# Attention and two MLPs on one core: load places given back earlier, more places, conversions planned further behind their loads

## The chip, the cores and the metric

One core of one Trainium2 chip runs the whole program: one launch, all inputs in HBM, the result back to HBM. The metric is the device time in microseconds (us), median over runs. TensorE (PE) multiplies, VectorE (DVE) and ScalarE (ACT) do element work, SyncE (SP) issues most DMAs, ACT issues the rest, GpSimd (POOL) does one reduction in the attention stage. Each engine works through its own instructions in program order.

## The reference

```python
def phi(x):
    proj = np.einsum('bhsd,df->bhsf', x, w_phi)
    proj = proj - np.max(np.abs(proj), axis=-1, keepdims=True)
    return np.concatenate([np.exp(proj), np.exp(-proj)], axis=-1)
q_p, k_p = phi(q), phi(k)                       # q, k, v: (4, 8, 576, 64), fp32; w_phi: (64, 128)
kv  = np.einsum('bhsf,bhsd->bhfd', k_p, v)
num = np.einsum('bhsf,bhfd->bhsd', q_p, kv)
den = np.einsum('bhsf,bhf->bhs', q_p, np.sum(k_p, axis=2))[..., None] + 1e-06
x = (num / den) as (2304, 512)
h = x @ moe_w_in;   x = np.maximum(0.01 * h, h) @ moe_w_out       # first MLP, 512 -> 2048 -> 512
h = x @ moe2_w_in;  g = h * np.tanh(softplus(h)); out = g @ moe2_w_out   # second MLP
```

The four MLP weights are float64 (the others are float32); the kernel turns them into float32 on the chip, as bit patterns.

## The kernel before

**Stages.** Attention comes first. Then the first product of the first MLP, here stage A: 8 pairs of 128 hidden rows (f = 0..7) times two halves of the tokens (sb), 16 items, each made in a Strassen-like form from seven block products. A product (`prod`, L677) is six matmuls of 128x512: every fp32 operand is split into a high and a low part, and three matmuls stand for one. `cycle(n)` (L953) writes out item n: seven products with a call of `work()` behind each. Behind each f comes `c_item`, the leftover tokens, with two more calls. Then the second product of the first MLP, stage B: 72 steps (`l2_step`), each two halves of six matmuls with a `work()` behind each (the eight steps of the leftover tokens have twelve matmuls of 256 columns a half). Then the second MLP, stage C.

**Weights.** A unit is 128 x 512 float64 numbers, 512 KB. `Loads.load` (L115) issues the next unit's DMA on SP into a load place, the tile `stage`, of which there are two, whenever one is free in the planner's books. `conversion` (L130) makes float32 of it: `clamp` (two DVE steps, L137 and L139), `scale` (one ACT step, L143), `join` (two DVE steps, L148 and L150); the load place is given on at the end of `join`. The result lies in one of three word places, tile `c`. Of the 64 units 7 are converted during attention, 31 in the order of stage A (`l1_order`: six pairs of the first MLP's input weights, and 19 others that are stored as float32 in HBM, `scr`, by `to_store`), and 26 in the order of stage B (`l2_order`: 16 of the second MLP's input weights that go straight into their final place, `direct`, and 10 that are stored). `from_store` fetches stored units back and splits them into their final place (`into_home`).

**The planner.** The order of the side work is fixed while the program is built. `work()` (L646) advances a counter of products, `pos`, adds `rate` to a budget of DVE microseconds, and lets up to four active chains (`Chain`, L620) each issue one stage if the budget is positive, the stage's `gate` is open and its `ok` holds. A chain at the head of the queue starts only when it may, and those behind it wait. `landed(u)` (L841) holds a conversion back until `LAND` = 3 products after its load was issued in the books; what the load then does on the chip the planner doesn't know. `need(mark)` issues work by force until a mark is reached, without heeding budget or `LAND`; `drain()` empties the queue by force, ahead of the last products of stage A and ahead of step 55 of stage B. A matmul that needs a DVE or ACT result stands behind whatever these engines were given earlier: the sum `g` of `tail5` (L747), `join_w` (L752), the copy `seed_y` (L700), and in stage B the low part `gl` (L95).

Of the kernel before, what the change touches and what calls it, by code (L numbers as in the profile page):

```python
# [10 lines left out]
F32 = mybir.dt.float32  # L11
# [12 lines left out]
def attention_two_mlps_kernel(  # L24
# [40 lines left out]
    CS, LAND = 3, 3  # L65
# [41 lines left out]

    class Loads:


        def __init__(self, units):
            self.units, self.at, self.stage, self.when, self.pos = units, 0, {}, {}, [0]

        def load(self, ahead=1):
            while self.at < len(self.units) and len(self.stage) <= ahead:  # L115
                which, m, x = self.units[self.at]
                self.at += 1
                stg = gp.tile([P, DM, 2], I32, tag="stage", name="stage")
# [8 lines left out]
                self.when[which, m, x] = self.pos[0]  # L127

    def conversion(u, then):

        box = {}

        def clamp():
            loads.load()
            stg = box["s"] = loads.stage[u]
            c = box["c"] = gp.tile([P, DM], F32, tag="c", name="c", bufs=CS)
            nc.vector.tensor_scalar(out=c, in0=stg[:, :, 1].bitcast(F32), scalar1=F64_TOP, scalar2=-F64_TOP,  # L137
                                    op0=ALU.min, op1=ALU.max)
            nc.vector.tensor_scalar(out=stg[:, :, 0], in0=stg[:, :, 0], scalar1=29, scalar2=None,  # L139
                                    op0=ALU.logical_shift_right)  # L140

        def scale():
            nc.scalar.activation(out=box["c"], in_=box["c"], func=AF.Copy, scale=2.0 ** -112)  # L143

        def join():
            stg, c = box["s"], box["c"]
            e = stg[:, :, 0]
            nc.vector.scalar_tensor_tensor(out=e, in0=stg[:, :, 1], scalar=-(1 << 31), in1=e,  # L148
                                           op0=ALU.bitwise_and, op1=ALU.bitwise_or)
            nc.vector.scalar_tensor_tensor(out=c.bitcast(I32), in0=c.bitcast(I32), scalar=3, in1=e,  # L150
                                           op0=ALU.logical_shift_left, op1=ALU.bitwise_or)
            del loads.stage[u]
            loads.load()
            then(c)

        return clamp, scale, join
# [7 lines left out]
    def fetch(u):  # L164
        c = gp.tile([P, DM], F32, tag="c", name="f", bufs=CS)
        nc.sync.dma_start(out=c, in_=scr[u])
        return c
# [74 lines left out]
    with tc.manual_schedule():  # L242
# [253 lines left out]
        def attention(n):  # L496
# [48 lines left out]
            if n == PAIRS - 1:  # L545
# [4 lines left out]
        ATT = {1: ((0, 0, 0), keep), 2: ((0, 1, 0), keep), 5: ((0, 0, 1), store), 7: ((0, 2, 0), keep),  # L550
               8: ((0, 3, 0), keep), 15: ((0, 1, 1), store), 16: ((0, 2, 1), store)}
        HERE, EARLY, EACH = 4, 1, 3
# [3 lines left out]
        for f in range(2, NF + 1):  # L556
# [13 lines left out]
            5: lambda: low(*w_all(0, 2, 3)),  # L570
# [7 lines left out]
            15: lambda: low(*w_all(1, 2, 3)),  # L578
# [10 lines left out]
        }  # L589

# [18 lines left out]
        gd, free, undone, pos, tokens, rate = {}, set(), set(), [0], [0.0], [1.3]  # L609
        queue, active, sent = [], [], []  # L610
        loads.pos = pos
# [34 lines left out]
        def work(force=False):  # L646
            pos[0] += 1
            while sent:
                sent.pop(0)()
            tokens[0] = min(tokens[0], 0.0) + rate[0]  # L650
            for x in list(active):
                x.step(force)
            active[:] = [x for x in active if x.stages]
            while queue and len(active) < 4 and not any(x.open() for x in active) and (force or queue[0].begin <= pos[0]):
                x, n = queue[0], len(queue[0].stages)
                x.at = -9
                x.step(force)
                if len(x.stages) == n:
                    return
                queue.pop(0)  # L660
                if x.stages:
                    active.append(x)

        def need(*mark):
            while mark in undone:
                work(True)
# [70 lines left out]
        def leaky(key, h, g=None):  # L737
            g = staged() if g is None else g
# [61 lines left out]

        c_part = lambda: cw + [XC]
        x1 = lambda o: (lambda: x_part(1, o))

        def row(cost, *todo, mark=None):
            def f():
# [22 lines left out]
              row(1.22, lo_(x1(T4)), mark=("x", 1, T4)))  # L828

        held = []

        def room(force=False):
            return len(held) < CS or held[-CS][0]

        def hold():
            held.append([False])
            return held[-1]

        def landed(u):  # L841
            def ok(force):
                loads.load()
                return room() and u in loads.stage and (force or pos[0] >= loads.when[u] + LAND)
            return ok

        def conv_stages(u, last=True):

            box = {}
            c, s, j = conversion(u, lambda x: box.update(out=x))  # L850

            def c_():
                box["h"] = hold()
                c()
            return box, [Stage(0.85, c_, ok=landed(u), last=last), Stage(0.0, s), Stage(1.38, j)]

        def drop(box, f=None):
            def g():
                if f is not None:
                    f()  # L860
                box["h"][0] = True
            return g

        def w_chain(f, begin):
# [13 lines left out]
            c1.after = 1  # L878
            chain(c0, Stage(0.85, both(s0.f, c1.f), ok=c1.ok, last=False), Stage(1.38, both(j0.f, s1.f)), Stage(1.38, both(j1.f, got)),
# [7 lines left out]
        def to_store(u):  # L887
            box, st_ = conv_stages(u)
            j = st_[2]
            f = j.f  # L890
            j.f = drop(box, lambda: (f(), store(u)(box["out"])))
            chain(*st_)
# [18 lines left out]
        def into_home(u, box):  # L911
            def h():
                home[u] = home_of(u)
                high(home[u] + [box["out"]])

            return [Stage(0.0, h), Stage(0.69, drop(box, lambda: low(home[u] + [box["out"]])), ("o",) + u)]
# [5 lines left out]
        def from_store(u, begin=0):  # L922
            box = {}

            def get():
                box["h"] = hold()
                box["out"] = fetch(u)
            h, l = into_home(u, box)
            h.after = LAND
            chain(Stage(0.0, get, ok=room, last=True), h, l, begin=begin)  # L930
# [76 lines left out]
        def load_g(s):  # L1007
# [4 lines left out]
            else:  # L1012
                if (s - LAST) % 2 == 0:
                    raw2[0] = gp.tile([P, 2, MAIN], F32, tag="stage", name="raw2")
# [113 lines left out]
        def mish(g, done):  # L1128
# [19 lines left out]
            if new:  # L1148
                if g % 2 == 0 or pair[0] is None:
                    pair[0] = gp.tile([P, 2, MAIN], F32, tag="stage", name="u")  # L1150
# [20 lines left out]
            if new:  # L1171
                r0 = gp.tile([P, MAIN], F32, tag="c", name="r", bufs=CS)
# [36 lines left out]
        for x in items[2:]:  # L1209
            if x[0] == "w" or n == 1:  # L1210
                cycle(n)
                n += 1
                if n == len(it) - 1:
                    for s in range(6):
                        load_g(s)
# [15 lines left out]
        splits(-1)  # L1231
        box2 = {}

        def swap(m):
# [3 lines left out]
            if m + CS < M:  # L1238
                box2[m + CS] = fetch(out2[m + CS])

        def l2_step(s):
            emit_y(s, 0, 1)
            work()
            emit_y(s, 2, 3)
            splits(s)
            if s < LAST + 4:
                load_g(s + 6)
            elif (s - LAST) % 2 == 0:
                load_g(s + 6)
                load_g(s + 7)  # L1250
# [4 lines left out]
        for s in range(NS):  # L1255
            if s == LAST - 1:
                drain()
            if s == LAST:
                for m in range(CS):
                    box2[m] = fetch(out2[m])  # L1260
# [45 lines left out]
```

## Time and profile before

| | |
|---|---|
| median of 3 runs | 1025.89 us (1025.8 to 1028.55) |
| the profiled execution | 1024.99 us, of which the trace's span is 1022.9 us |
| PE busy | 962.8 us, 94% |
| DVE busy | 722.6 us, 71% |
| ACT busy | 529.8 us, 52% |
| POOL busy | 68.7 us, 7% |
| DMA | 108.11 MB, 106 GB/s over the span |
| chain that ended last, by engine | PE 55%, DMA 16%, DVE 12%, issue 2%, ACT 1% |
| stage A, first to last matmul | 182.5 to 394.0 us |
| stage B up to its last conversions | 394.0 to about 550 us |

The busy shares are means over stages with different limits, so the stages are to be read one by one. A busy PE is one with a matmul in flight; it can run at the full or at half of its clock, which the row PEclk tells.

### The profile page before, as it was taken

What the parts mean: (1) busy time and instruction counts of PE and PEld (TensorE: products, weight loads), DVE (VectorE), ACT (ScalarE), POOL (GpSimd) and SP (SyncE); (2) the same over time, 40 slices, a digit from 0 to 9 for tenths busy, and PEclk for the clock granted to TensorE, in tenths of its full rate; (3) what the DMA queues carried; (4) which work ended last, traced back from release to release, by engine and by line L of the source; (5) the groups of instructions that cost most, each with busy time, mean ns of one, the idle gap of its engine ahead of it and who ended that gap; (6) DMA issues with size and microseconds to landing.
All of it is one profiled execution on the core that took longest, in us unless ns stands there. A gap on an engine that the chain in (4) does not pass through costs nothing.

```text
span 1022.9 us, 16911 instructions
## 1 busy us (share of the span) xinstructions
PE 962.8 (94%) x6645; PEld 810.4 (79%) x6645; DVE 722.6 (71%) x1282; ACT 529.8 (52%) x898; POOL 68.7 (7%) x36
## 2 busy tenths in 40 slices
PE   8999999997888879888799999999999999999998
PEld 7889998775776768766687887888888988888886
DVE  7888996765666624675665355978876888868976
ACT  6888886653544434443423344545544555545543
POOL 4434341000000000000000000000000000000000
PEclk9999999998998989999998999999999999999999
DMA  7524411265666775555576361000100100001001
GB/s 197 141 74 136 130 46 48 100 221 190 202 215 214 236 252 187 165 170 177 153 242 215 106 184 31 1 1 1 42 1 1 42 1 21 1 1 42 1 0 42
DMA packets 87246, 108.11 MB, mean 106 GB/s; under 512 B 29312, under 2 KB 54272, under 8 KB 87168
## 3 DMA queue, kind: packets, MB, share of 16 engines
q1 hardware_dynamic: 65696, 68.90, 22.6%
q10 hardware_dynamic: 21472, 38.15, 11.2%
q8 instruction: 52, 0.85, 0.3%
q14 instruction: 26, 0.21, 0.1%
HBM read 75.04 MB, written 31.98 MB: 105 GB/s over the span
## 4 chain that ended last, share of the span: by engine, by line
PE 55%; DMA 16%; DVE 12%; issue 2%; ACT 1%; ACTq 0%; DVEq 0%; SPq 0%
PE a L98 9%; PE a L100 9%; PE b L98 9%; PE a L99 9%; PE b L100 9%; PE b L99 9%; DMA stage<-in_moe_w_in_dram 8%; DMA stage<-in_moe_w_out_dram 7%; DVE stage L148 3%; DVE c L150 2%; DMA f<-scr 2%; DVE gl L95 1%; PE outs L434 1%; DVE stage L139 1%; DVE c L199 1%
## 5 line engine op out<-in xcount | busy, mean ns | idle before, releaser
L100 PE MATMUL a<-win,wi 128*128 128x512 f32 (+1 forms) x320 | 117.7, 368 | 0.0
L99 PE MATMUL a<-win,wi 128*128 128x512 f32 (+1 forms) x320 | 117.7, 368 | 0.0
L98 PE MATMUL a<-win,wi 128*128 128x512 f32 (+1 forms) x320 | 117.7, 368 | 0.0
L100 PE MATMUL b<-wo,gl 128*128 128x512 f32 x288 | 112.3, 390 | 1.0 <-DVE gl L1164 1.0
L98 PE MATMUL b<-wo,gh 128*128 128x512 f32 x288 | 112.2, 389 | 0.0
L99 PE MATMUL b<-wo,gh 128*128 128x512 f32 x288 | 112.1, 389 | 0.0
L143 ACT ACTIVATE c<-c 128x512 f32<-128x512 f32 x64 | 40.4, 632 | 101.9 <-DVE c L137 99.8
L95 DVE TENSOR_TENSOR gl<-raw,gh 128x512 fp32r<-128x512 f32 x72 | 49.5, 689 | 58.6 <-ACT gh L94 51.2
L137 DVE TENSOR_SCALAR c<-stage 128x512 f32<-128x512 f32 x64 | 27.2, 424 | 85.7 <-DMA stage<-in_moe_w_in_dram 48.9
L1146 ACT ACTIVATE gh<-u 128x512 fp32r<-128x512 f32 x72 | 45.5, 633 | 70.7 <-PE b L99 63.9
L99 PE MATMUL b<-gl,wo 128*128 128x512 f32 (+1 forms) x192 | 69.7, 363 | 7.0 <-DVE gl L95 7.0
L394 POOL PARTITION_ALL_REDUCE qm<-qd x32 | 68.5, 2189 | 90.8 <-ACT qd L389 77.2
L1173 ACT ACTIVATE r<-e,two 128x512 f32<-128x512 f32 x72 | 51.7, 718 | 36.2 <-DVE e L1158 36.2
L100 PE MATMUL b<-gh,wo 128*128 128x512 f32 (+1 forms) x192 | 69.3, 361 | 0.0
L98 PE MATMUL b<-gh,wo 128*128 128x512 f32 (+1 forms) x192 | 69.2, 360 | 0.0
L94 ACT ACTIVATE gh<-raw 128x512 fp32r<-128x512 f32 x72 | 43.5, 623 | 49.3 <-PE b L100 21.8
L98 PEld LDWEIGHTS a<-win,wi 128*128 128x128 f32 x320 | 60.3, 188 | 10.3
L99 PEld LDWEIGHTS a<-win,wi 128*128 128x128 f32 x320 | 60.3, 188 | 10.3
L100 PEld LDWEIGHTS a<-win,wi 128*128 128x128 f32 x320 | 60.3, 188 | 10.0
L1142 ACT ACTIVATE e<-a 128x512 f32<-128x512 f32 x72 | 43.0, 597 | 47.8 <-PE a L100 26.6
L99 PE MATMUL a<-gl,wo 128*128 128x512 f32 x128 | 53.5, 418 | 11.9 <-DVE gl L95 11.8
L100 PEld LDWEIGHTS b<-wo,gl 128*128 128x128 f32 x288 | 54.1, 188 | 13.0 <-DVE gl L1164 1.8
(219 smaller groups left out, 2391.7 us busy)
## 6 DMA issues: line engine op xcount, KB each, us to landing
gd<-g ACTq DMA_DIRECT2D x72, 256.0 KB, 2.8
raw<-gd ACTq DMA_DIRECT2D x72, 256.0 KB, 3.0
stage<-in_moe_w_in_dram SPq DMA_DIRECT2D x32, 512.0 KB, 4.5
stage<-in_moe_w_out_dram SPq DMA_DIRECT2D x32, 512.0 KB, 4.4
scr<-c SPq DMA_DIRECT2D x32, 256.0 KB, 4.8
f<-scr SPq DMA_DIRECT2D x32, 256.0 KB, 2.9
qn<-in_q_dram SPq DMA_DIRECT2D x16, 256.0 KB, 4.5
vmain<-in_v_dram SPq DMA_DIRECT2D x32, 128.0 KB, 3.0
```

The lines of the kernel that those rows point to most:

```text
L94: nc.scalar.activation(out=hi, in_=src, func=AF.Copy)
L95: nc.vector.tensor_tensor(out=lo, in0=src, in1=hi.bitcast(F32), op=ALU.subtract)
L98: nc.tensor.matmul(out=o, lhsT=wh_, rhs=xh, start=start, stop=False, **kw)
L99: nc.tensor.matmul(out=o, lhsT=wh_, rhs=xl, start=False, stop=False, **kw)
L100: nc.tensor.matmul(out=o, lhsT=wl_, rhs=xh, start=False, stop=stop, **kw)
L137: nc.vector.tensor_scalar(out=c, in0=stg[:, :, 1].bitcast(F32), scalar1=F64_TOP, scalar2=-F64_TOP, op0=ALU.min, op1=ALU.max)
L143: nc.scalar.activation(out=box["c"], in_=box["c"], func=AF.Copy, scale=2.0 ** -112)
L148: nc.vector.scalar_tensor_tensor(out=e, in0=stg[:, :, 1], scalar=-(1 << 31), in1=e, op0=ALU.bitwise_and, op1=ALU.bitwise_or)
L394: nc.gpsimd.partition_all_reduce(qm, qd, P, bass_isa.ReduceOp.absmax)
L1142: nc.scalar.activation(out=e0, in_=h0, func=AF.Exp)
L1146: nc.scalar.activation(out=hi2, in_=u2, func=AF.Copy)
L1173: nc.scalar.activation(out=r0, in_=e0, func=AF.Ln, bias=two)
```

## The change

The load place is given on at the end of `clamp` instead of `join`: for conversions in the stages A and B the step L148 (the low bits) moves into the same stage and writes into a second word place instead of back into the load place; the next load is issued right there. Two more load places and four more word places are cut out of tiles that held the tokens of the second half (`x2`, `x3`), from the time that those are split until product 98 (the load places until 84), and single tiles are lent later (`lh`, `a7`). A conversion needs two open word places. `LAND` goes from 3 to 6. The rates go from 1.3 to 1.15 (stage A) and from 1.0 to 0.9 (stage B). The `drain()` at the end of the cycles and the later queueing of stage B's units go: all chains are queued at once, with gates on places that stage A still uses. Some ACT and DMA issues are put one or two products later, and in stage B `splits` comes between the two halves of a step.

```diff
-    CS, LAND = 3, 3
+    CS, LAND = 3, 6
+    class Places:            # keeps the books of load and word places
+        def open(self, of):
+            return [x for x in of if x.tile is None and self.pos[0] < x.until]
+        def room(self, n):
+            return len(self.open(self.words)) >= n
+        def closed(self, close):
+            return self.pos[0] >= close and not any(x.close == close and x.tile is not None for x in self.words + self.stages)
...
+        def low_bits():
+            stg = box["s"]
+            e = box["e"] = places.take(places.words) if early else stg[:, :, 0]
+            nc.vector.scalar_tensor_tensor(out=e.bitcast(I32) if early else e, in0=stg[:, :, 1], scalar=-(1 << 31),
+                                           in1=stg[:, :, 0], op0=ALU.bitwise_and, op1=ALU.bitwise_or)
+            if early:
+                loaded()
+        def loaded():
+            places.drop(loads.stage.pop(u))
+            loads.load()
...
+            if early:
+                low_bits()                     # at the end of clamp()
...
-            del loads.stage[u]                 # at the end of join()
-            loads.load()
+            if early:
+                places.drop(e)
+            else:
+                loaded()
...
-            sent.append(lambda: nc.scalar.dma_start(out=gd[key], in_=g))
+            later(1, lambda: nc.scalar.dma_start(out=gd[key], in_=g))
...
-            leaky((2 * x["f"] + 1, 2 * x["sb"] + 1), c, c)
+            later(1, lambda: leaky((2 * x["f"] + 1, 2 * x["sb"] + 1), c, c))
...
+        def more_places():
+            for x in range(2):
+                t = place("x2_%d" % x, F32, 2, DM, name="more")
+                places.words += [places.Word(lambda t=t, i=i: t[:, i], CLOSE) for i in range(2)]
+                places.stages.append(places.Word(lambda x=x: place("x3_%d" % x, I32, DM, 2, name="stage"), CLOSE, CLOSE - 14))
...
-                return room() and u in loads.stage and (force or pos[0] >= loads.when[u] + LAND)
+                return places.room(n) and u in loads.stage and (force or pos[0] >= loads.when[u] + LAND)
...
-            return box, [Stage(0.85, c_, ok=landed(u), last=last), Stage(0.0, s), Stage(1.38, j)]
+            return box, [Stage(1.53, c, ok=landed(u), last=last), Stage(0.0, s), Stage(0.69, j)]
...
-            h.after = LAND
+            h.after = LAND - 2                 # a fetched unit
...
+            chain(*st_, Stage(0.0, drop(box), after=LAND - 1))     # a stored unit keeps its word place
...
-            from_store(out1[m])
+            from_store(out1[m], CLOSE)
+        for u in out1[HERE:]:
+            from_store(u)
+        for u in l2_order:
+            (to_store if u[2] == 1 else direct)(u)
...
-                free.update((it[n]["f"], i) for i in parts)
+                later(2, lambda: free.update((it[n]["f"], i) for i in parts))
...
-        drain()
-        for u in out1[HERE:]:
-            from_store(u)
-        for u in l2_order:
-            (to_store if u[2] == 1 else direct)(u)
...
-        rate[0] = 1.0
+        rate[0] = 0.9
...
             emit_y(s, 0, 1)
+            splits(s - 1)
             work()
             emit_y(s, 2, 3)
-            splits(s)
```

## Rows read from the trace of the kernel before

**Rows 1.** The page: forty slices of the span, PE busy and granted clock, in tenths.
```profile
PE   8999999997888879888799999999999999999998
PEclk9999999998998989999998999999999999999999
```

**Rows 2.** Stretches by stage: busy us and instructions of each engine, PEclk, DMA share, GB/s.
```profile
182.50:394.00 211.50, 184.09 (x829) 148.52 (x830) 124.56 (x223) 100.07 (x171) 0.00 (x0) 0.94 0.62 204
394.00:550.00 156.00, 135.99 (x634) 111.93 (x633) 98.86 (x180) 60.26 (x106) 0.00 (x0) 0.93 0.60 185
550.00:640.00 90.00, 89.04 (x393) 73.43 (x392) 42.38 (x67) 35.00 (x59) 0.00 (x0) 1.00 0.41 121
640.00:1022.90 382.90, 379.21 (x1762) 317.04 (x1760) 306.32 (x516) 189.95 (x304) 0.00 (x0) 1.00 0.04 13
```

**Rows 3.** PE's waits in stage A: us in total, times, longest.
```profile
PE b L98 <- ACT b L700: 10.4, 4, 5.2
PE b L98 <- DVE g L747: 7.9, 4, 2.9
PE a L98 <- ACT x L203: 4.7, 2, 4.0
PE b L98 <- DVE b L752: 1.9, 4, 1.1
PE a L100 <- DVE a L207: 1.4, 1, 1.4
PE a L100 <- DVE x L207: 1.0, 2, 0.6
```

**Rows 4.** PE's waits from 394 to 550 us, stage B.
```profile
PE a L99 <- DVE gl L95: 11.8, 8, 3.2
PE b L99 <- DVE gl L95: 7.0, 3, 3.5
PE a L98 <- ACT gh L94: 1.2, 1, 1.2
```

**Rows 5.** DVE's waits from 180 to 405 us, the longest two.
```profile
DVE c L137 <- DMA stage<-in_moe_w_in_dram: 26.2, 10, 3.6
DVE c L137 <- DMA stage<-in_moe_w_out_dram: 20.3, 12, 2.6
```

**Rows 6.** DVE's waits from 405 to 550 us, the longest two.
```profile
DVE c L137 <- DMA stage<-in_moe_w_in_dram: 22.7, 7, 4.5
DVE c L137 <- DMA stage<-in_moe_w_out_dram: 16.5, 9, 3.0
```

**Rows 7.** The tile stage: conversion steps (ns, min/median/max) and its loads' landing.
```profile
L137 DVE TENSOR_SCALAR c<-stage x64: 417/426/431, 23.3 to 547.6; 128x512 f32<-128x512 f32 x64
L139 DVE TENSOR_SCALAR stage<-stage x64: 420/422/427, 23.6 to 548.0; 128x512 int32<-128x512 int32 x64
L148 DVE SCALAR_TENSOR_TENSOR stage<-stage x64: 683/686/702, 30.9 to 550.3; 128x512 int32<-128x512 int32 x64
L150 DVE SCALAR_TENSOR_TENSOR c<-c,stage x64: 691/693/698, 31.6 to 551.0; 128x512 int32<-128x512 int32 x64
...
DMA to landing us min/median/max: 3.5/4.4/7.6
```

**Rows 8.** Timeline of DVE, stage B: start, us, line, [idle before, releaser].
```profile
431.28 0.43 DVE L137 TENSOR_SCALAR c<-stage 128x512 f32<-128x512 f32 x1 [4.49 <-DMA stage<-in_moe_w_in_dram]
...
487.07 0.43 DVE L137 TENSOR_SCALAR c<-stage 128x512 f32<-128x512 f32 x1 [3.36 <-DMA stage<-in_moe_w_in_dram]
```

**Rows 9.** Timeline of PE, stage A.
```profile
198.29 0.39 PE L98 MATMUL a<-s,a 128*128 128x512 f32 x1
...
203.05 0.39 PE L98 MATMUL b<-s,a 128*128 128x512 f32 x1
...
370.11 0.80 PE L98 MATMUL b<-v,x 128*128 128x512 f32 x1 [5.19 <-ACT b L700]
```

**Rows 10.** The stretch of 25 us with most DMA.
```profile
350.00:375.00 25.00, 19.81 (x90) 16.32 (x89) 13.39 (x24) 10.00 (x19) 0.00 (x0) 0.87 0.82 265
```

More of the change, by code (lines that the diff above doesn't have):

```diff
@@ L106, in attention_two_mlps_kernel, with __init__, take, drop @@
     scr = {}
+    class Places:
+        class Word:
+            def __init__(self, make, close=1 << 20, until=None):
+                self.make, self.close, self.until, self.tile, self.since = make, close, until or close, None, 0
+        def __init__(self):
+            self.pos, self.clock = [0], 0
+            self.words = [self.Word(lambda i=i: place("c%d" % i, F32, DM, pool=gp, name="c")) for i in range(CS)]
+            self.stages = [self.Word(lambda i=i: place("st%d" % i, I32, DM, 2, pool=gp, name="stage")) for i in range(2)]
+        def open(self, of):
[4 more added lines that the diff above has]
+            return self.pos[0] >= close and not any(x.close == close and x.tile is not None for x in self.words + self.stages)
+        def take(self, of):
+            x = min(self.open(of), key=lambda x: x.since)
+            x.tile = x.make()
+            return x.tile
+        def drop(self, t):
+            x = [x for x in self.words + self.stages if x.tile is t][0]
+            self.clock += 1
+            x.tile, x.since = None, self.clock
+    places = Places()
     class Loads:
         def __init__(self, units):
-            self.units, self.at, self.stage, self.when, self.pos = units, 0, {}, {}, [0]
-        def load(self, ahead=1):
-            while self.at < len(self.units) and len(self.stage) <= ahead:
+            self.units, self.at, self.stage, self.when = units, 0, {}, {}
+        def load(self):
+            while self.at < len(self.units) and places.open(places.stages):
                 which, m, x = self.units[self.at]
                 self.at += 1
-                stg = gp.tile([P, DM, 2], I32, tag="stage", name="stage")
+                stg = places.take(places.stages)
                 if x == 0:
@@ L126, in load, with conversion @@
                 self.stage[which, m, x] = stg
-                self.when[which, m, x] = self.pos[0]
-    def conversion(u, then):
+                self.when[which, m, x] = places.pos[0]
+    def conversion(u, then, early=False):
         box = {}
+        def low_bits():
[8 more added lines that the diff above has]
+            loads.load()
         def clamp():
@@ L162, in store, with fetch @@
         return f
-    def fetch(u):
-        c = gp.tile([P, DM], F32, tag="c", name="f", bufs=CS)
+    def fetch(u, at=None):
+        c = places.take(places.words) if at is None else place("c%d" % at, F32, DM, pool=gp, name="f")
         nc.sync.dma_start(out=c, in_=scr[u])
@@ L589, in attention_two_mlps_kernel, with free_pair @@
         }
+        def free_pair(f):
+            for i in range(2):
+                places.drop(kept.pop((0, 2 * f + i, 0)))
         def extra(n, at):
@@ L797, in attention_two_mlps_kernel @@
         head2(0)
+        def more_places():
[3 more added lines that the diff above has]
+                places.stages.append(places.Word(lambda x=x: place("x3_%d" % x, I32, DM, 2, name="stage"), CLOSE, CLOSE - 14))
+        places.words.append(places.Word(lambda: place("lh", F32, DM, pool=late[0], name="more"), CLOSE2))
         c_part = lambda: cw + [XC]
@@ L860, in g @@
                     f()
-                box["h"][0] = True
+                places.drop(box["out"])
             return g
@@ L1149, in mish @@
                 if g % 2 == 0 or pair[0] is None:
-                    pair[0] = gp.tile([P, 2, MAIN], F32, tag="stage", name="u")
+                    pair[0] = place("st%d" % (g // 2 % 2), F32, 2, MAIN, pool=gp, name="u")
                 u0 = pair[0][:, g % 2]
@@ L1230, in attention_two_mlps_kernel @@
         c_item(NF - 1, lambda: (tail3(n - 1), work()), work)
-        splits(-1)
+        work()
+        free.add("l1")
+        places.words.append(places.Word(lambda: place("a7", F32, DM, name="more")))
         box2 = {}
```

88 lines of the change are left out of this document (43 added, 45 removed).

## The prediction

> **What bounds the kernel now.** I read the slices of the page first. PE is full from the 24th slice on and at full clock there; the thin place is the middle, slices 7 to 22, where its share falls to 7 or 8 tenths and the granted clock dips too [rows 1]. By stages: from 550 us on PE is busy 468.3 of 472.9 us at clock 1.00, so nothing outside PE can shorten that; stage A (211.5 us) has clock 0.94, stage B's first part (156 us) 0.93 [rows 2]. So the loss lies in these two, and I ask the waits of PE there. In A they sum to 10.4 + 7.9 + 4.7 + 1.9 + 1.4 + 1.0 = 27.3 us [rows 3], in B to 11.8 + 7.0 + 1.2 = 20.0 us [rows 4]. All name an ACT or DVE step as releaser. One step back, DVE: in the same stretches it stood 26.2 + 20.3 = 46.5 us [rows 5] and 22.7 + 16.5 = 39.2 us [rows 6] at one instruction, L137, the first step of a conversion, waiting for its load. DVE works in order, so the sum, join or low part that PE needs was queued behind a conversion written out before its load had landed. ACT's `seed_y` comes late the same way: it stands behind a `scale` that waits for that L137. DVE is not full: 124.6 of 211.5 us and 98.9 of 156 us [rows 2].
>
> A product is short beside a load. Matmuls start (203.05 - 198.29) / 21 = 0.227 us apart [rows 9], so six are 1.36 us, and `LAND` = 3 products are 4.1 us. A load lands 3.5 to 7.6 us after its issue, median 4.4 [rows 7], and its issue on the chip comes later than in the books, since it waits for the `join` before it. More than half are late by construction.
>
> There is a second bill. In the same slices the granted clock falls below 1 [rows 1], that is, PE spends part of them at the lower of its two levels (1.2 instead of 2.4 GHz). The clock of 0.94 over 211.5 us is 0.06 x 211.5 = 12.7 us lost in A, and 0.07 x 156 = 10.9 us in B [rows 2]. So what stands above an unhindered PE is 27.3 + 12.7 = 40.0 us in A and 20.0 + 10.9 = 30.9 us in B, 70.9 us in all; the span could fall to 1022.9 - 70.9 = 952 us, and no further, since the rest is PE's.
>
> **The change, part by part.**
>
> *Six products instead of three.* Six are 8.2 us, above the longest landing seen, 7.6 us [rows 7]. Since the next load's issue is now written right behind the last reader of its place, the eight microseconds count from the issue itself, not from the books two stages earlier. Where a conversion is not forced, L137 no longer waits. That removes the cause of the 85.7 us of DVE's waits [rows 5, 6]; PE's gain is only its own 70.9.
>
> *Load place back after L148.* The DVE work per unit stays the same four steps, 0.426 + 0.422 + 0.686 + 0.693 = 2.23 us [rows 7], and so does the planner's price (0.85 + 1.38 before, 1.53 + 0.69 after). L148 now writes a dense word place and L150 reads one; the trace has no such row, so bounds: between 0.42 (the single-input steps L137, L139) and 0.70, that is a gain of at most 57 x 2 x 0.27 = 31 us of DVE time, or a loss of nothing. I take no change, as these are two-input steps of the same size, and neither lies on the path once DVE has idle time. What moves is 0.69 us from one product to another: the stage becomes one run of 0.43 + 0.42 + 0.69 = 1.53 us, which can delay a waiting `g` or `gl` by up to 1.53 us. PE asks for `g` two products (2.7 us) after it could be made, so this hides. If that cover is gone (DVE already behind by over 1.2 us), it costs up to 0.7 us a conversion.
>
> *How fast units can go then.* With `LAND` = 6 a load place turns round in six products, 8.2 us. In B there are two places, so a unit each 4.1 us. Before, ten units between the two rows of stage B took 487.07 - 431.28 = 55.8 us, 5.6 us each [rows 8]. So the longer hold is still a faster loop, as the wait and the two stages of holding are gone. 26 units take 107 us. They start when the twelve fetched units ahead of them are through (four of them at a time, four to six products each, the first four fetched ahead), some 14 products or 19 us into B, and so end at 126 us; the `drain()` ahead of step 55 stands at 55 x 2 x 1.36 = 150 us. In A, 31 units in 15 x 7 + 7 x 2 + 5 = 124 products are one per four; four places allow one per 1.5, two allow one per 3. Both suffice.
>
> *Rates.* By the planner's prices A needs about 31 x 2.22 + 6 x 4.18 for the parts of six pairs + 16 for the tokens' splits + 3 for four fetched units = 113 us of DVE, and 124 products at 1.15 give 143. B needs 26 x 2.22 + 28 x 0.69 = 77 us, 86 products at 0.9, of 110 up to the drain. So the lower rates make nothing late by themselves, and DVE gets at most 1.15 + 1.3 / 7 = 1.34 us per product of 1.36, the sums of a cycle included.
>
> *The drain at the end of A goes.* It forced fetches in a row; PE's longest wait in A, 5.19 us at 370.11, lies there [rows 9] and is in the 40 us already. *ACT's issues a product later, `splits` between the halves:* same instructions, off the path; nothing, within 1 us either way per stage.
>
> *DMA.* The same bytes. A moves 204 GB/s x 211.5 us = 43 MB [rows 2]; in 180 us that is 240 GB/s at a share of about 0.73. The densest stretch did 265 GB/s at 0.82 [rows 10], so there is room. But up to four loads can be in flight. Scaling that stretch to a full share, 265 / 0.82 = 323 GB/s, four loads of 524 KB take 6.5 us; still under 8.2. Here a rule of the Trainium skill speaks against the change: "DMA: Bandwidth & Descriptors", section "Issuing engines are not separate DMA queues", says that all DMAs end on the same 16 engines and interleave, so more of them in flight bring no more bandwidth and each lands later. With that page's limit of HBM per core, 358 GB/s (its "Specifications"), four loads would be an estimated 5.9 us. No row of before shows how four loads share; by that estimate, too, the sum stays as it is, as 5.9 us is under six products.
>
> *Sum.* I do not take all 70.9. Small waits of the chain PE-ACT-DVE-PE within a cycle stay, a few loads land late beside stores, and each long remainder brings some half clock. I choose that a fifth stays: 8 of 40 in A, 6 of 31 in B. Gain 57 us: span 1022.9 - 57 = 966, with the 2.1 us around the span 968. The profiled execution lies 0.9 us under the median, so the median is 969 us.
>
> **The rivals.**
>
> 1. *Only A gains.* B keeps two load places, and its conversions, `gl` and fetches share one DVE. If units run late there, `drain()` forces the rest and PE waits as before. For it: half of B's gain hangs on 24 us of slack before the drain. Against: the turn of 4.1 us against 5.6. Time: 1025.9 - 32 = 994.
>
> 2. *Loads stretch each other in A.* Four in flight, beside stores and `gd`, land after 8 us instead of 4.4, so L137 waits on. For: the median landing of 4.4 us is for two places. Against: the bytes are the same, and the 6.5 us above. The rule of the Trainium skill cited above would have it so, if its estimate were larger. Only B gains: 1025.9 - 25 = 1001.
>
> 3. *It doesn't do what it says.* The books run ahead of the chip; word places run out (each conversion needs two, a stored one keeps its word for seven products), and `need` forces the steps of before. DVE then waits at L137 as now: 1026.
>
> 4. *Slower: the pairs of stage A come late.* A pair needs four open words at once, and it must be complete when its item's first product is written out. If stored units hold the words, `need` forces the pair with nothing beside it: a load of 4.4 us, two conversions of 2.23 and a split of about 1.2, some 10 us, plus about 2 us of half clock behind so long a wait. Six pairs make 72 us against a gain of 57: 1041. It decides from the fifth pair on. For: two of the lent places close at product 98, load places at 84, before the last pair is done. Against: a pair starts 14 to 19 products (19 to 26 us) ahead of its need, and up to seven words are open then.
>
> **How the numbers follow.** Forecast 0.64 (969, its own range 955 to 982); rival 1 0.14 (994), rival 2 0.08 (1001), rival 3 0.06 (1026), rival 4 0.08 (1041). The floor is 952 + 3 = 955. The range runs from 954 to 1004: it holds the forecast, both half gains, and leaves out rivals 3 and 4 with 0.14 and some of the forecast's tails. The DVE bounds shift nothing in it, as DVE is off the path where loads are in time, and its 0.7 us a conversion (57 x 0.7 = 40 us, if every one is exposed) stays within it. About 0.3%, 3 us, is what a measurement tells from no change: faster 0.86 (forecast, rivals 1 and 2), same 0.06, slower 0.08.
>
> **What would show it.** Right: L137's waits for the load fall from 46.5 and 39.2 us to under 10 together; PE's waits in A and B to some 15 us; the granted clock to 0.98 or more in both; A about 180 us and B's conversions with PE full; from the first product of the second MLP on, all as before. Landing times up to 8 us and no `drain` stall ahead of step 55. Wrong: L137 still waits in A (rival 2), only in B (rival 1), or PE waits at the first product of an item for a weight's low part (rival 4).

## The result, and the profile after

The changed kernel takes 953.44 us (median of 4 runs, 952.49 to 955.93) against 1025.85 us, a ratio of 0.9298 (95% interval 0.9267 to 0.9328). The forecast was 969 with a range of 954 to 1004: the direction was right, the gain larger than forecast (72.4 us against 57), and the median lies 0.6 us under the range.

The page of the kernel after: span, slices of PE and its clock, and the chain that ended last, by engine.

```profile
span 954.0 us, 16891 instructions
PE   8999999999999989999999999999999999999998
PEclk9999999999999989999999999999999999999999
PE 85%; ACT 1%; DVE 1%; DMA 0%; issue 0%; ACTq 0%; DVEq 0%
```

The thin stretch of [rows 1] is gone but for one slice, the 15th. DMA and DVE, 16% and 12% of the chain before, are at 0% and 1%. The stretches of the kernel after, with the columns of [rows 2], cut where stage A ends (357.8 us) and at the last wait of PE (570.6 us):

```profile
182.50:357.80 175.30, 171.09 (x828) 144.31 (x829) 124.39 (x223) 99.57 (x170) 0.00 (x0) 0.98 0.75 251
357.80:550.00 192.20, 192.20 (x938) 163.08 (x937) 129.72 (x226) 86.69 (x149) 0.00 (x0) 1.00 0.66 202
570.60:954.00 383.40, 379.66 (x1762) 317.57 (x1762) 306.70 (x516) 190.19 (x305) 0.00 (x0) 1.00 0.04 13
```

Stage A took 211.5 us [rows 2] and takes 175.3: 36.2 us won. Its DVE work is the same, 124.4 us. PE is busy all through stage B. Both kernels have a last wait of PE, for the second MLP's first `gl`; here it is before and after, in the timeline of PE (start, us, line, [idle before, releaser]).

```profile
639.54 0.50 PE L100 MATMUL b<-wo,gl 128*128 128x512 f32 x1 [0.96 <-DVE gl L1164]
```

```profile
570.65 0.50 PE L100 MATMUL b<-wo,gl 128*128 128x512 f32 x1 [0.95 <-DVE gl L1223]
```

From there to the end both take 383.4 us (1022.9 - 639.54, 954.0 - 570.65), so nothing was won in stage C. Stage B up to there went from 639.5 - 394.0 = 245.5 to 570.6 - 357.8 = 212.8 us: 32.7. Together 68.9 us, the difference of the two spans. (The medians differ by 72.4: the profiled execution after lies 2.5 us above its median, the one before 0.9 under.) The waits of PE in stage A that are left (in stage B there is none up to that last one), against [rows 3, 4]:

```profile
PE b L98 <- DVE g L808: 2.5, 1, 2.5
PE b L98 <- ACT b L760: 1.3, 1, 1.3
PE a L98 <- ACT x L253: 0.4, 1, 0.4
```

And DVE's wait for loads, which was 85.7 us [rows 5, 6], with the landing times of the loads ([rows 7] before):

```profile
DVE c L182 <- DMA stage<-in_moe_w_out_dram: 0.6, 1, 0.6
...
DMA to landing us min/median/max: 3.6/4.5/7.1
```

Over all loads the landing is no shorter than before. In stage A its median even rose, from 4.5 to 5.1 us, as more loads are in flight. What changed is when loads are issued and when they are asked for.

### The profile page after: what moved, and what is told of

Same layout as the page of the kernel before. It is cut to its first block, busy times and chain, and to the rows that moved or that the text cites. A ratio compares the mean times of both kernels' runs of the same rounds, so it can differ in the third digit from the quotient of the medians.

```text
span 954.0 us, 16891 instructions
## 1 busy us (share of the span) xinstructions
PE 937.2 (98%) x6645; PEld 800.6 (84%) x6645; DVE 722.4 (76%) x1282; ACT 530.0 (56%) x898; POOL 68.7 (7%) x36
## 3 DMA queue, kind: packets, MB, share of 16 engines
q10 hardware_dynamic: 21472, 38.15, 11.9%
## 4 chain that ended last, share of the span: by engine, by line
PE 85%; ACT 1%; DVE 1%; DMA 0%; issue 0%; ACTq 0%; DVEq 0%
PE b L98 14%; PE b L100 14%; PE b L99 14%; PE a L98 14%; PE a L100 13%; PE a L99 13%; PE outs L484 1%; PE kvp L461 1%; DMA gd<-g 0%; PE a L377 0%; PE xt L509 0%; PE kvp L464 0%; PE kvp L513 0%; ACT g L800 0%; PE outs L489 0%
## 5 line engine op out<-in xcount | busy, mean ns | idle before, releaser
L1232 ACT ACTIVATE r<-e,two 128x512 f32<-128x512 f32 x72 | 51.7, 718 | 36.1 <-DVE e L1217 36.1
L98 PE MATMUL b<-gh,wo 128*128 128x512 f32 (+1 forms) x192 | 68.2, 355 | 0.0
L100 PE MATMUL b<-gh,wo 128*128 128x512 f32 (+1 forms) x192 | 68.0, 354 | 0.0
L98 PEld LDWEIGHTS b<-wo,gh 128*128 128x128 f32 x288 | 54.1, 188 | 11.1
L99 PEld LDWEIGHTS b<-wo,gh 128*128 128x128 f32 x288 | 54.1, 188 | 10.9
L1223 DVE TENSOR_TENSOR gl<-u,gh 128x512 fp32r<-128x512 f32 x72 | 49.5, 688 | 9.2 <-ACT gh L1205 9.2
```

What stands on the lines that cost most here:

```text
L98: nc.tensor.matmul(out=o, lhsT=wh_, rhs=xh, start=start, stop=False, **kw)
L99: nc.tensor.matmul(out=o, lhsT=wh_, rhs=xl, start=False, stop=False, **kw)
L100: nc.tensor.matmul(out=o, lhsT=wl_, rhs=xh, start=False, stop=stop, **kw)
L1223: nc.vector.tensor_tensor(out=lo2, in0=u2, in1=hi2.bitcast(F32), op=ALU.subtract)
L1232: nc.scalar.activation(out=r0, in_=e0, func=AF.Ln, bias=two)
```

## Experiments

The theory behind the forecast, D: six products between load and conversion take the waits away. Its rival, R: the rate at which load places come free. The first four runs test them; after them come other theories, as each was needed. All medians are against the kernel before on the same chip (1024.4 to 1026.1 us). "DVE" is DVE's waits for loads and "PE" all waits of PE, from 182 us to the end of stage B, in one profiled run each; the kernel before has 85.7 and 48.3, the kernel after 0.6 and 5.2.

| run | what | median us | ratio (95%) | DVE | PE |
|---|---|---|---|---|---|
| e1 | before, six products | 1010.21 | 0.984 (0.982 to 0.987) | 36.1 | 42.8 |
| e2 | after, three products | 953.94 | 0.930 (0.928 to 0.932) | 3.2 | 4.9 |
| e3 | after, two load places | 966.70 | 0.942 (0.940 to 0.944) | 3.4 | 15.1 |
| e4 | after, place back at join | 961.83 | 0.937 (0.935 to 0.939) | 4.6 | 11.2 |
| e5 | e2 and e3 | 957.90 | 0.936 (0.934 to 0.939) | 21.0 | 8.6 |
| e6 | e2 and e4 | 952.08 | 0.930 (0.927 to 0.932) | 3.2 | 4.2 |
| e7 | e2, e3 and e4 | 958.43 | 0.937 (0.935 to 0.939) | 10.8 | 8.3 |
| e8 | e7, old rates | 955.77 | 0.934 (0.932 to 0.936) | 16.1 | 6.1 |
| e9 | e8, conversion's old form | 1015.63 | 0.991 (0.988 to 0.994) | 81.2 | 44.6 |
| e10 | e9, three words | 1017.93 | 0.994 (0.991 to 0.996) | 84.0 | 48.2 |
| e11 | e10, drain back | 1018.11 | 0.993 (0.991 to 0.995) | 85.2 | 46.0 |
| e12 | after, splits later | 950.07 | 0.928 (0.924 to 0.931) | 0.3 | 2.7 |
| e13 | e8, low bits in place | 977.61 | 0.953 (0.951 to 0.956) | 43.2 | 18.9 |
| e14 | e8, low bits in join | 966.21 | 0.941 (0.938 to 0.944) | 28.5 | 12.8 |
| e15 | after, conversion's old form | 954.16 | 0.930 (0.927 to 0.933) | 33.2 | 5.6 |
| e16 | e9, new prices | 978.24 | 0.954 (0.952 to 0.955) | 42.5 | 21.5 |
| e17 | e9, two words in the books | 1006.19 | 0.982 (0.979 to 0.984) | 72.0 | 40.4 |
| e18 | before, new prices | 1000.47 | 0.975 (0.974 to 0.977) | 53.8 | 34.6 |

### The distance alone, and without it (e1, e2)

```diff
-  ... (force or pos[0] >= loads.when[u] + LAND)      # e1, in the kernel before
+  ... (force or pos[0] >= loads.when[u] + 6)
-  ... (force or pos[0] >= loads.when[u] + LAND)      # e2, in the changed kernel
+  ... (force or pos[0] >= loads.when[u] + 3)
```

> The kernel before with one number changed: a conversion waits for six products behind its load's issue, not three; two load places, given back at the end of join. Theory D (the distance between load and conversion is what took DVE's waits away, places matter little): DVE's waits for loads fall from 46.5 and 39.2 us to under 15 together, time 960 to 975, what stays being the two drains. Theory R (the rate of the loads matters as much): a place now turns in six plus two products, a unit per four products or 5.4 us, which is no faster than the 5.6 us of before; units fall behind, the drains and the weights' needs force them, waits at L137 come back in lumps there; 985 to 1020.

> The changed kernel with the distance put back to three products (4.1 us), all else as changed. Theory D: a load lands 4.5 us (median) behind its issue and three products are 4.1, so most of 57 conversions wait 0.5 to 3 us; DVE's waits for loads are 40 us or more and the time 970 to 1000. Theory R: the places carry the change, the waits stay under 15 us, time under 960.

e1 gains 15.6 us of 72, e2 loses nothing. So six products are not needed in the changed kernel, and alone they are not enough for the whole gain: D is wrong as the cause. R's range for e1 (985 to 1020) holds. But the two stages of e1 differ (columns of [rows 2], cut at the end of stage A and at PE's last wait):

```profile
182.50:411.30 228.80, 187.79 (x832) 150.93 (x831) 126.07 (x224) 101.82 (x171) 0.00 (x0) 0.88 0.57 189
411.30:623.60 212.30, 211.40 (x1023) 178.51 (x1022) 140.93 (x246) 95.89 (x165) 0.00 (x0) 1.00 0.60 187
```

Stage B takes 212.3 us, as in the changed kernel (212.8): there the distance alone brings the whole gain, and PE waits nowhere between 420 and 620 us. Stage A takes 228.8 us, 17.3 more than before. Its waits of PE lie elsewhere than before (timeline of PE):

```profile
247.82 0.80 PE L98 MATMUL a<-v,x 128*128 128x512 f32 x1 [7.80 <-ACT x L203]
250.38 0.80 PE L100 MATMUL a<-v,x 128*128 128x512 f32 x1 [1.33 <-DVE x L207]
253.65 0.80 PE L98 MATMUL a<-v,x 128*128 128x512 f32 x1 [1.21 <-ACT x L203]
```

These are the first products of an item, waiting 10.3 us in all for weights that come late; three such rows come again from 308 and from 369 us on. It is the place of the forecast's rival 4 and its 10 us of waiting, in a kernel where a load place turns in eight products; the half clock with it (0.88 over the stage, 0.94 before) costs more than the 2 us a pair put there.

### Places and their return in the books (e3 to e8)

```diff
-                places.stages.append(places.Word(lambda x=x: place("x3_%d" % x, ...), CLOSE, CLOSE - 14))   # e3
-                loaded()          # e4: at the end of low_bits()
+            loaded()              # e4: at the end of join(), always
-  tokens, rate = [0.0], [1.15]    ...    rate[0] = 0.9      # e8
+  tokens, rate = [0.0], [1.3]     ...    rate[0] = 1.0
```

> The changed kernel without the two lent load places: two places throughout, given back behind L169, six products. Theory D: two places turned in six products give a unit per three products, and stage A needs one per four; time 953 to 958. Theory R: stage A loses the loads in flight; a pair and the three stored units behind it come late, need forces them, time 965 to 985.

> The changed kernel with the load place given back at the end of join (two products later) instead of behind L169; four places up to product 84, then two, six products. Theory D: 953 to 960, a unit per two products in A; in B a unit per four products, so that some two to four of 26 are left for the drain ahead of step 55, which forces them for a few us. Theory R: stage B runs at 5.4 us a unit like before and PE waits there again, 970 to 990.

e3 met R's range by its lower end: pairs come late near 245 us (6.4 us of PE's waits), and the last wait of stage A grew from 2.5 to 4.9 us. e4 fell between the two ranges: 8 us longer, of which 5.4 + 0.9 us are two waits of PE at 518 to 520 us, the forced units ahead of step 55 that D had put at "a few us".

> The changed kernel with two load places and three products; early give-back and all else as changed. After the first runs: distance did nothing while four places were there. Theory B (the books: in stage B the budget, 0.9 us a product against 2.91 us a unit, spaces the loads by itself; in stage A spare places do): stage B stays free of waits; stage A has forced pairs as with two places and six products, or fewer since a conversion may start sooner; 955 to 968. Theory D' (with two places a load is fresh when it is used, so distance binds): DVE waits 1 to 2 us at most conversions of A, over 25 us in all, time 975 or more.

> The changed kernel with three products and the load place given back at the end of join; four places. Theory B: four places still let loads run ahead in A, so A is as changed; in B a place given back two products or more later turns more slowly, some units are left for the drain ahead of step 55, or L137's successor waits; 955 to 965. Theory D': waits in B as in the kernel before, about 39 us of DVE's and 20 of PE's; 980 or more.

> The changed kernel with its three named parts put back together: two load places, three products, give-back at the end of join. What is left of the change are the word places, the lower rates, the queue without the drain and the later issues. If the three parts carry the gain: waits of DVE for loads over 60 us, time 1000 to 1026. If the rest carries much of it: 970 to 995.

> As the one before it, and the old rates 1.3 and 1.0 too. If the rates space the loads (theory B), the waits of DVE for loads grow by 10 us or more over those with the lower rates, time 5 to 20 us longer; if they don't matter, the two agree within 3 us.

With three products instead of six, two places cost 4 us (e5; 7 by the ratios, as the chips differ) and the late return nothing (e6); with six they cost 13 and 8 (e3, e4). All three parts put back in the planner's books, and the old rates with them, the kernel still takes 955.77. So the parts that the change is named after, as the books have them, are not needed for the gain, nor are the lower rates; D' is wrong, and theory B, which had the rates space the loads, is wrong on e8. e6 and e7 came out below both of their ranges.

### The conversion's form (e9 to e11)

```diff
-            c, s, j = conversion(u, lambda x: box.update(out=x), True)      # e9
+            c, s, j = conversion(u, lambda x: box.update(out=x))
-  [Stage(1.53, c, ok=landed(u), last=last), Stage(0.0, s), Stage(0.69, j)]   # landed: two open words
+  [Stage(0.85, c, ok=landed(u), last=last), Stage(0.0, s), Stage(1.38, j)]   # landed: one
...                                # e10: more_places, lh and a7 are not lent; e11: also
+        drain()                   # behind the cycles, stage B's chains queued after it
```

> The kernel of e8 (two load places, three products, give-back at join, old rates) and also the old form of the conversion: the low bits are made in join, back into the load place, at the old prices, one word a conversion; eight word places and the queue without the drain stay. Theory S (the step's place and its second word: a conversion that needs two words starts alone, so loads no longer come in pairs): waits of DVE for loads come back, over 40 us, time 975 to 1000. Theory W (word places and the queue carry it): within 5 us of e8, 951 to 961.

> As e9 with three word places only, as in the kernel before (none lent). A pair of stage A holds two of three for 10 products or more, so what is stored goes through one word, seven products each. Theory W: the pairs come late, need forces them, 985 to 1020, PE's waits in A at the first product of an item. If words don't matter: within 5 us of e9.

> As e10 with the drain back at the end of the cycles and stage B's units queued behind it: close to the kernel before but for the later issues, the gates and the order of gl. Theory Q (the drain and the forced needs behind it put stage B's conversions into pairs): stage B gets its 16 to 20 us of PE waits back, 15 to 35 us slower than e10. If the drain matters only by its own stall: 5 to 10 us slower than e10. Against the kernel before: within 10 us of 1025 if nothing else of the change counts.

This is the step: e9 is 60 us longer than e8, more than theory S had asked, and has nearly all the waits of the kernel before. Words and drain are worth nothing beyond it here (1015.6, 1017.9, 1018.1), so W and Q fall. The forecast laid PE's longest wait in stage A to the drain; putting the drain back (e11) adds no time.

### Which half of the form (e13, e14, e16 to e18), and the parts as a makeweight (e15)

```diff
-            e = places.take(places.words)                        # e13: the word is taken in the books only
+            e = stg[:, :, 0]
-            if early: low_bits()       # e14: moved from the end of clamp() to join(), still into the second word
-  Stage(0.85, ...), ..., Stage(1.38, j)                          # e16 in e9; e18 in the kernel before
+  Stage(1.53, ...), ..., Stage(0.69, j)
-        def landed(u, n=1):                                      # e17 in e9, a second word in the books
+        def landed(u, n=2):
```

> The kernel of e8 with one operand moved: the low bits are made in the clamp stage as there, but back into the load place, so join reads the load place last, two products later. The books (two words a conversion, prices, order) are those of e8. Theory C (on the chip a load is released by the last step that reads its place, not by the books): DVE's waits for loads go from 16 to 60 us or more, 1000 to 1020. Theory S (the second word and the prices space the conversions): as e8, 952 to 960.

> The kernel of e8 with the low bits made in join, into the second word, which is taken in clamp as before: same books, same words, the step two products later in DVE's order. Theory C: the load place is read last in join, so 1000 to 1020, waits 60 us or more. Theory S: 952 to 960.

> e9 with the new prices only (first stage 1.53, last 0.69), the instructions unchanged. If the price spaces the conversions (one first stage empties the budget of a product, 1.3, so that the next conversion can't start in the product behind it): stage B's first steps come singly, DVE's waits for loads fall from 81 us to 30 to 50, time 965 to 990. If not: 1010 to 1020.

> e9 with two words a conversion in the books only (the second is not used), old prices, the instructions unchanged. If the second word spaces them (four words in stage B hold one conversion at its start at a time): waits of 30 to 50 us, 965 to 990. If not: 1010 to 1020.

> The kernel before with the new prices only. If the price alone breaks up the pairs there too: stage B loses most of its 20 us of PE waits, 985 to 1010. If the three words held in a ring make the pairs: 1015 to 1028.

Both halves are real: the step that reads the load place last, and the prices with the second word. With the books of e8 and join as the last reader of the load place, 10 us (e14) or 22 us (e13) are lost (8 and 20 by the ratios): less than theory C asked, but clear of S's 952 to 960. The timelines of DVE and SP in e8 show the release itself:

```profile
420.11 0.69 DVE L169 SCALAR_TENSOR_TENSOR c<-stage 128x512 int32<-128x512 int32 x1
420.83 0.37 SPq L158 DMA_DIRECT2D stage<-in_moe_w_in_dram  x1
422.05 0.68 DVE L195 SCALAR_TENSOR_TENSOR c<-c 128x512 int32<-128x512 int32 x1
```

The next load goes out 0.03 us after the low bits (L169) end, and 1.2 us ahead of join's step (L195), behind which the books of e8 give the place back.

And e16, with the instructions of e9 and two prices changed, wins 37 us. The price does it by the order. These are conversions in stage B of the kernel before, from DVE's timeline, and the two loads behind the first pair, with their landing:

```profile
438.40 0.42 DVE L137 TENSOR_SCALAR c<-stage 128x512 f32<-128x512 f32 x1
...
441.84 0.43 DVE L137 TENSOR_SCALAR c<-stage 128x512 f32<-128x512 f32 x1 [2.68 <-DMA stage<-in_moe_w_in_dram]
...
449.93 0.42 DVE L137 TENSOR_SCALAR c<-stage 128x512 f32<-128x512 f32 x1
```

```profile
L125 SPq DMA_DIRECT2D stage<-in_moe_w_in_dram x1: 368/368/368, 434.1 to 434.1; - x1
DMA to landing us min/median/max: 3.5/3.5/3.5
...
L125 SPq DMA_DIRECT2D stage<-in_moe_w_in_dram x1: 369/369/369, 436.0 to 436.0; - x1
DMA to landing us min/median/max: 5.7/5.7/5.7
```

The first steps of conversions in stage B of e9:

```profile
420.41 0.42 DVE L180 TENSOR_SCALAR c<-stage 128x512 f32<-128x512 f32 x1
...
423.74 0.43 DVE L180 TENSOR_SCALAR c<-stage 128x512 f32<-128x512 f32 x1 [1.97 <-DMA stage<-in_moe_w_in_dram]
...
430.87 0.42 DVE L180 TENSOR_SCALAR more<-stage 128x512 f32<-128x512 f32 x1
...
433.82 0.43 DVE L180 TENSOR_SCALAR c<-stage 128x512 f32<-128x512 f32 x1 [1.60 <-DMA stage<-in_moe_w_in_dram]
```

and the same stretch of e16:

```profile
420.33 0.42 DVE L180 TENSOR_SCALAR c<-stage 128x512 f32<-128x512 f32 x1
...
425.06 0.42 DVE L180 TENSOR_SCALAR c<-stage 128x512 f32<-128x512 f32 x1
...
429.57 0.42 DVE L180 TENSOR_SCALAR more<-stage 128x512 f32<-128x512 f32 x1
...
433.74 0.43 DVE L180 TENSOR_SCALAR c<-stage 128x512 f32<-128x512 f32 x1 [0.50 <-DMA stage<-in_moe_w_in_dram]
```

In e9, as in the kernel before, two conversions start some 3 us apart and then none for 7 or 8. Their places come free together, their loads go out together (1.9 us apart above), and the second is asked for before it has landed. A pair also stretches its second load: of the 55 loads after 182 us in the kernel before, 24 go out less than 3 us behind another, and these land after 5.7 us (median), the 24 ahead of them after 4.1. In e16 conversions come singly, every 4.5 us; 29 of its loads go out alone, landing after 4.2 us, and a load has the whole turn of the other place to land in. The price of 1.53 empties the budget of a product, so that the next conversion cannot start right behind; that this is how the price works is argued from the planner's code, that the price does it is shown. The second word in the books wins 9 us at the old prices (e17, between its two ranges) and nothing at the new ones (e13, which has it, takes 977.6, e16 978.2). The prices alone, put into the kernel before, win 25 us (e18).

> The changed kernel with only the conversion's form put back (low bits in join, into the load place, old prices, one word); four load places, six products, eight words, new rates. Theory C with distance as its makeweight: six products cover a release two products late (8.2 - 2.7 = 5.5 us against a landing of 4.5), so waits are small, and units run late for the turn of eight products; 958 to 980. If places and distance are worth nothing: as e9, 1005 to 1020.

With the other parts of the change in place, the old form costs nothing: 954.16, under both ranges. In stage A, where it has four load places, DVE's waits go (3.0 us, against 50.7 in e9). In stage B they do not: there e15 has two load places like e9, its loads go out in pairs, and DVE waits 30.2 us, as in e9 (30.5). But PE waits only 1.0 us for `gl` in that stage, and in e9 15.3. One such place of e15, from DVE's timeline:

```profile
429.98 1.29 DVE L95 TENSOR_TENSOR gl<-raw,gh 128x512 fp32r<-128x512 f32 x2
...
436.71 0.43 DVE L182 TENSOR_SCALAR c<-stage 128x512 f32<-128x512 f32 x1 [4.77 <-DMA stage<-in_moe_w_in_dram]
```

Two `gl` are made ahead of the wait; around the waits of e9 they come one at a time, between the conversions. That this keeps the wait from PE is argued, and which part of e15 puts them ahead was not tried.

So what e8 has is enough: the conversion's form, with the eight words, the queue without the drain and the later issues around it. What e15 has is enough too: the old form, with four places, six products, the eight words and the lower rates among the rest. The form alone, in the kernel before, was not run. Undone singly neither shows; undone together, with words and drain, they give the kernel before back to within 8 us (e11).

### The last wait (e12)

In the kernel after, DVE and then PE at the end of stage A:

```profile
351.22 0.69 DVE L95 TENSOR_TENSOR gl<-raw,gh 128x512 fp32r<-128x512 f32 x1 [2.91 <-DMA gd<-g]
351.83 0.68 DVE L808 TENSOR_TENSOR g<-b,z 128x512 f32<-128x512 f32 x1
```

```profile
352.56 0.80 PE L98 MATMUL b<-s,x 128*128 128x512 f32 x1 [2.50 <-DVE g L808]
```

The sum `g` stands behind a `gl` whose data come back from HBM.

```diff
-        splits(-2)
         stage_tags[0] = ("ta",)
...
         tail5(n - 1)
+        splits(-2)
         work()
```

> The changed kernel with the first split of stage A's stored results put behind tail5's sum at the end of stage A. The one wait of PE of over 2 us that is left in A and B (2.5 us at 352.6, behind a gl that waits for its DMA) goes, with the half clock behind it: 1 to 4 us faster than the changed kernel, 949 to 953. If the wait only moves to the first gl of stage B: no change, 952 to 955.

950.07 us (949.98 to 950.57): 3.4 us under the kernel after, and the runs of the two don't overlap, though they were not timed side by side and the intervals of their ratios do. PE's waits in A and B:

```profile
PE b L98 <- ACT b L760: 1.3, 1, 1.3
PE b L100 <- DVE gl L1223: 1.0, 1, 1.0
PE a L98 <- ACT x L253: 0.4, 1, 0.4
```

The wait is gone and did not move. This version is faster than the kernel before and, by these runs, a little faster than the kernel after.

## Why the prediction was right in direction and short in size

**Where the loss lay: right.** Stages A and B gave 36.2 and 32.7 us, stage C nothing. L137's successor waits 0.6 us, the granted clock is 0.98 and 1.00, and the last conversion's first step starts at 486.3 us, 128 us into stage B where 126 was worked out. The step that now writes a word place takes 0.69 us as before, which was taken without a row. (The slices were misread: the thin stretch of [rows 1] begins at the 10th, not the 7th. Nothing was worked out from that.)

**The term that failed: "I choose that a fifth stays: 8 of 40 in A, 6 of 31 in B".** No row stood behind it. In B nothing stayed (no wait, clock 1.00), so the 6 us were wrong; in e1's stage B PE waits nowhere from 420 us on either, so the small waits of a chain PE-ACT-DVE-PE that I kept there came with the loads. In A 4.2 us of waits and 0.02 x 175.3 = 3.5 us of clock stayed, 7.7 in all: there the 8 came out, by luck. B won 32.7 us against the 25 forecast and A 36.2 against 32, which is 11.9 of the gain that was missing; the rest lies between the spans and the medians. What A won above its 32 is about what the next point gives (17 waits at 0.28 us, 4.8 us).

**"The span could fall to 952 us, and no further": mis-sized too.** e12 has a span of 948.1 us. A wait costs more than the idle time booked for it. In the kernel before (timeline of PE):

```profile
340.25 0.39 PE L100 MATMUL a<-v,a 128*128 128x512 f32 x1
343.53 0.50 PE L98 MATMUL b<-s,x 128*128 128x512 f32 x1 [2.89 <-DVE g L747]
343.87 0.40 PE L99 MATMUL b<-s,x 128*128 128x512 f32 x1
```

From the first of these starts to the third are 3.62 us where two steps of 0.227 [rows 9] would be 0.45: 3.17 us lost, 2.89 booked. Counted in the same way, 23 of the 30 waits from 182 to 640 us cost 0.26 to 0.28 us more than is booked, and the other seven more still. My reading is that the overlap of matmuls (0.39 us long, 0.227 apart) has to build up again. At 0.28 us each, the 17 waits of [rows 3] and 12 of [rows 4] hide another 8 us, which puts the floor at an estimated 944; e12, with 2.7 us of waits left, stands 4 above it.

**"Six products instead of three ... removes the cause": wrong as a cause.** It is enough by itself in stage B, where e1 has the whole gain, and makes stage A 17.3 us longer there; in the changed kernel it is not needed at all (e2). I took the planner's hold for the chip's: the books say when a load may be written out, but on the chip its issue waits for the last step that reads the place. When L148 moved into the clamp stage, that came earlier whatever the books said (e8's load goes out right behind L169; e6 against e2: no loss; e13 against e8: 22 us). And I costed the two prices at nothing, as their sum stays 2.22. They set the order, and the order made the pairs.

**The rivals.** Rival 1 (only A gains) did not come: no unit was forced ahead of step 55; where the place came back late (e4) that drain did cost 6.3 us. Rival 3 (the planner forced as before) did not come. Rival 4 did not come in the changed kernel, and did in e1. Rival 2's mechanism did come, but not its price. The densest stretch of the kernel after moves more than any of before [rows 10]:

```profile
225.00:250.00 25.00, 24.64 (x119) 20.23 (x118) 21.10 (x42) 14.10 (x25) 0.00 (x0) 1.00 0.91 306
```

The loads issued there landed after 5.3 us (median; at most 6.5), those of before's densest stretch after 5.0, and no wait of L137's successor lies there. The Trainium skill ("DMA: Bandwidth & Descriptors", "Issuing engines are not separate DMA queues") says that DMAs run on the same 16 engines and interleave. The trace agrees in that a load issued close behind another lands later (5.7 against 4.1 us in the pairs of the kernel before). The forecast's further step, that more in flight bring no more bandwidth, the trace does not bear out (306 against 265 GB/s in the densest stretches).

**Open.** Why e11 is 8 us faster than the kernel before was not followed up; the later issues, the gates and the moved `splits` are what is left between them. (Q had asked for 15 to 35 us between e10 and e11, and there are none.) Which of word places and load places holds the pairs of stage A back in e1 was not tried, nor which part of e15 keeps DVE's waits from PE.

## What to carry to other kernels

In these kernels a load is released by the last instruction that reads its buffer, so move the last reader forward before adding buffers, and read in the trace which step it is. Where side work is spread by a budget, look at the starts of its first steps: two close together and then a gap meant paired loads here, the second of which lands late, and a price pulled them apart without changing an instruction. Undoing one part of a change that brings no loss does not show that the part was idle; undo the others too.

## What was not expected of the hardware

A wait of PE cost about 0.28 us more than the idle time that the profile books for it (3.17 against 2.89 above). Of two loads issued within 3 us of each other the second took 1.6 us longer to land than the first (5.7 against 4.1 us in the kernel before). DVE's waits for loads are no price by themselves: e15 has 33.2 us of them, the kernel after 0.6, and both take the same time.
